# Keys and values on 128 partitions with 64x64 matmul tiles, filler matmuls and a rearranged start, in a kernel of efficient attention followed by a multiplicative feed-forward network

## The chip, the core and the metric

The kernel runs on one core of a Trainium2 chip; the other cores are idle. The metric is the device time of that core in microseconds (us), and a kernel's time is the median of its runs. The kernel before takes 279.56 us (three runs, 279.26 to 280.37). In the profiles, PE is the matrix engine (TensorE), PEld its weight loads, DVE is VectorE, ACT ScalarE, POOL GpSimd, and SP the engine that issues the DMA transfers. One-core kernels have no undisturbed second die to compare with, so a run counts as slow when it is over 1.5% above the fastest run of the same kernel; only fast runs are compared.

## The reference

Eight batches of eight heads with 576 tokens and a head dimension of 64 go through an attention without a token-by-token product: the queries get a softmax over the head dimension, the keys a softmax over the tokens, and `kv` is a 64x64 matrix for each head. Its output (4608 tokens of 512) goes through a feed-forward network of two matrices that are multiplied element by element, and two more matrices after that.

```python
def _attn_ref(q, k, v):                       # [8, 8, 576, 64] float32 each
    q_s = np.exp(q - np.max(q, axis=-1, keepdims=True))
    q_s = q_s / (np.sum(q_s, axis=-1, keepdims=True) + 1e-09)
    k_s = np.exp(k - np.max(k, axis=2, keepdims=True))
    k_s = k_s / (np.sum(k_s, axis=2, keepdims=True) + 1e-09)
    kv = np.einsum('bhsd,bhse->bhde', k_s, v)
    return np.einsum('bhsd,bhde->bhse', q_s, kv)

def _moe_ref(x, w1, w2, w3, w_out):           # x: [4608, 512]
    a = x @ w1                                # [4608, 1024]
    b = x @ w2
    h = a * b @ w3
    return h @ w_out                          # [4608, 512]
```

(Shortened; the types are unchanged.)

## The kernel before

The program is one list of tasks. Each task names its engine, a duration, what it depends on and which buffers it uses. When the kernel is built, a planner simulates all engines with these durations, takes for every engine the task that can start first (with priorities), gives out the buffers, and emits the instructions in that order. The order is then fixed: each engine's queue holds its instructions in the planned order. So a wrong duration or a wrong load rate in the plan does not make a wrong result; it can make an order in which an engine waits for something late while other work would be ready.

The two last matrices are multiplied once into `W3O` (called so below), since `h` is not needed. The first 512 tokens go through the feed-forward network plainly ("the plain group"). The other 4096 tokens are five groups of 2x320 to 2x448 tokens, each multiplied in a scheme with seven instead of eight block products. That needs combinations of the weight blocks (`make_w12`) and of the token blocks (`t_comb`).

Queries, keys and values are loaded on 96 partitions (each holds 6 consecutive tokens of 4 heads), in halves of 4 heads:

```python
    def load_qkv(b, which, hf):
        src = {"q": q, "k": k, "v": v}[which]
        load((which, b, hf), SP * 1536 * 4, 300.0,           # SP = 96, R = 6
             lambda t: t[:SP].rearrange("p (h x) -> p h x", h=4),
             src[b, 4 * hf:4 * hf + 4].rearrange("h (p r) d -> p h (r d)", r=R))
```

`load` takes one of six staging buffers (`st`) of 128x1536 float32, for all loads, weights too. The loads are issued in program order, so a staging buffer that is held long stops everything behind it.

Keys get an exp on ACT, values a cast on POOL, and a batch's `kv` is 24 matmuls of 96 rows with two heads side by side (off-diagonal blocks are computed and thrown away). Queries get an exp on ACT, a sum on DVE, a multiplication on POOL into a further buffer, and a transpose: on PE for the first two batches, by DMA for the others.

```python
            def norm(eq=eq, ds=ds, eqn=eqn):                 # POOL
                nc.gpsimd.tensor_tensor(
                    out=eqn.tile..., in0=eq.tile..., in1=ds.tile[:, 1]..., op=ALU.mult)
        # ...
        def kvm():
            for hf in range(2):
                for g in range(2):
                    ek, v16 = eks[2 * hf + g][1].tile, v16s[hf][1].tile
                    o = 512 * hf + 130 * g
                    for r in range(R):
                        nc.tensor.matmul(
                            pa.tile[:, o:o + 130].rearrange("p (h e) -> p h e", h=2),
                            lhsT=ek[:, r].rearrange("p h d -> p (h d)"),
                            rhs=v16[:, 2 * g:2 * g + 2, r, 0:65],
                            start=(r == 0), stop=(r == R - 1))
```

(`...` marks cuts.) All of attention's PSUM goes through one tile, `tiles("pa", 1, [P, 1024], F32, psum)`. The weight combinations are made on DVE from the float32 staging buffers, so that those stay held until the combinations are done:

```python
        def k1():                                            # sw: float32, 2 buffers
            nc.vector.tensor_tensor(out=s1.tile, in0=a21, in1=a22, op=ALU.add)
        def k2():
            nc.vector.tensor_tensor(out=s2.tile, in0=s1.tile, in1=a11, op=ALU.subtract)
        # k3, k4 on DVE from a11, a12, a21 and s2; k5, k6 copy s1 and s2 to f16 on ACT
        # ...
        tt, ts = t_comb(i, 8.0 * i - 4, "DVE" if i == 1 else "POOL")
```

The softmax here doesn't subtract the row's maximum and nothing guards it: scores larger than these inputs give would overflow.

## Time and profile before

| reading | value | view |
|---|---|---|
| span of the profiled run | 279.1 us | head of the page |
| PE busy, over the whole span | 84% | busy time by engine |
| first matmul of the feed-forward network | 53.2 us | instructions on the tile `px` |
| first matmul of the second token group | 90.2 us | the same |
| from there to the end | 188.9 us | difference |
| last load of queries issued | 165.1 us | instructions of that load |
| chain of waits | 52% PE, 28% DMA | chain of waits |

The first view is from the page of the kernel before: its head, the busy time by engine, and three rows of the span cut into 40 slices of 7 us (PE busy share in tenths, granted clock in tenths, GB/s moved by DMA).

```profile
span 279.1 us, 4087 instructions
...
PE 234.3 (84%) x1344; PEld 122.1 (44%) x1344; DVE 164.2 (59%) x302; ACT 164.0 (59%) x298; POOL 145.2 (52%) x120
...
PE   1586862799946999894999995999999999999992
...
PEclk9999795599995799998899999999999999999999
...
GB/s 246 377 249 257 248 278 173 196 270 264 253 262 311 230 229 236 217 212 244 290 223 282 242 213 243 253 80 40 80 40 42 71 40 75 64 49 74 42 144 120
```

PE is 80 to 100% busy from the second quarter on, with dips. In the slice from 42 to 49 us PE drops to 2, and the clock is at 5 from 42 to 56 us; a second dip (4 and 6) follows from 77 to 91 us, with the clock at 5 in its second half. The loads run at about 250 GB/s until about 180 us, except in the second slice, where only weights are loaded (377), and around 42 to 56 us (173 and 196), where the loads themselves stall.

The next view cuts out four stretches. The columns are the stretch, its length, then for PE, PEld, DVE, ACT and POOL the busy us (and instructions), then the granted clock, the DMA share and GB/s.

```profile
15.00:39.00 24.00, 18.70 (x126) 8.91 (x125) 5.75 (x10) 10.84 (x15) 6.05 (x5) 0.93 1.08 250
42.00:54.00 12.00, 5.07 (x28) 2.72 (x28) 10.89 (x19) 7.88 (x15) 5.73 (x3) 0.52 0.50 165
60.00:63.00 3.00, 3.00 (x15) 1.37 (x14) 3.00 (x6) 3.00 (x6) 0.00 (x0) 1.00 1.09 259
90.20:182.00 91.80, 82.39 (x510) 45.54 (x509) 63.97 (x130) 71.83 (x138) 71.88 (x55) 0.96 1.12 239
```

In the stretch 60 to 63 us only keys and values are loaded, and the DMA is fully busy (share 1.09) at 259 GB/s. From 42 to 54 us the DMA share falls to 0.50 and PE works for 5 of 12 us at half the clock. From 90.2 to 182 us PE is idle for 91.80 - 82.39 = 9.4 us.

The next two views are the shares of the chain that ended last, and the matmuls on the tile `px` (columns: line, engine, operation, tiles and count; shortest, median and longest ns; first and last start in us; shapes). Line 568 is the seven-product scheme, line 509 the plain group.

```profile
PE 52%; DMA 28%; DVE 6%; ACT 4%; issue 4%; POOL 3%; SPq 0%; DVEq 0%; ACTq 0%; POOLq 0%
```

```profile
L568 PE MATMUL px<-xt,w x80: 296/352/474, 90.2 to 258.0; 128*128 128x448 f16 x48, 128*128 128x320 f16 x16, 128*128 128x384 f16 x16
...
L509 PE MATMUL px<-xt,w x32: 379/379/631, 53.2 to 66.5; 128*128 128x512 f16 x32
```

The last view shows three groups of instructions that the change touches (columns: line, engine, operation, tiles, shapes, count; busy us and mean ns of one; idle time of the engine before them and what ended it).

```profile
L306 DVE TENSOR_REDUCE ds<-eq 96x12 f32<-96x768 f16 x32 | 29.8, 930 | 6.7 <-ACT eq L300 6.6
...
L351 PE MATMUL pa<-v,ek 96*128 96x130 f16 x192 | 13.9, 231 | 1.2 <-ACT xt L388 0.7 <-POOL v L289 0.5
...
L544 POOL TENSOR_TENSOR tt<-xt 128x896 f16<-128x896 f16 x6 | 11.2, 1881 | 0.4 <-ACT xt L388 0.4
```

They are the sums of the queries, the kv matmuls (231 ns each in the mean, over 192 of them), and the token combinations on POOL, 1.88 us for one.

### The profile page before, as it was taken

The page shows a single profiled execution, that of the slowest core. Times are in us where ns is not written, and L with a number is a line of the kernel's source. Part 1 is how long each engine was busy: PE and PEld are TensorE (multiplying, and loading weights), DVE is VectorE, ACT ScalarE, POOL GpSimd, SP SyncE. Part 2 cuts the span into 40 slices and gives each one's busy share as a digit, 9 for nine tenths or more (in the row PEclk, how much of TensorE's full clock was granted, in tenths as well). Part 3 has the DMA queues.
Part 4 walks back from the last instruction along what each step waited for, and adds up shares of the span by engine and source line. Part 5 has one row for each costly group of instructions (what it writes and reads, how often), then busy time and mean ns, then how long its engine had stood idle before and what let it go on. Part 6 is the DMA issues. An engine that isn't in the chain of part 4 may idle for free.

```text
span 279.1 us, 4087 instructions
## 1 busy us (share of the span) xinstructions
PE 234.3 (84%) x1344; PEld 122.1 (44%) x1344; DVE 164.2 (59%) x302; ACT 164.0 (59%) x298; POOL 145.2 (52%) x120
## 2 busy tenths in 40 slices
PE   1586862799946999894999995999999999999992
PEld 1232331345424566541464542554544445555540
DVE  1210169983739779671798861898665565555510
ACT  3043546696755769776888685975645444545310
POOL 2213246204566378869869689989694221222200
PEclk9999795599995799998899999999999999999999
DMA  7999995699999999999999999931311212212154
GB/s 246 377 249 257 248 278 173 196 270 264 253 262 311 230 229 236 217 212 244 290 223 282 242 213 243 253 80 40 80 40 42 71 40 75 64 49 74 42 144 120
DMA packets 46037, 52.04 MB, mean 186 GB/s; under 512 B 16832, under 2 KB 39360, under 8 KB 46016
## 3 DMA queue, kind: packets, MB, share of 16 engines
q1 hardware_dynamic: 46016, 51.79, 77.0%
q8 instruction: 10, 0.16, 0.3%
q14 instruction: 11, 0.09, 0.1%
HBM read 38.80 MB, written 9.44 MB: 173 GB/s over the span
## 4 chain that ended last, share of the span: by engine, by line
PE 52%; DMA 28%; DVE 6%; ACT 4%; issue 4%; POOL 3%; SPq 0%; DVEq 0%; ACTq 0%; POOLq 0%
PE px L568 18%; PE pp L634 14%; PE pp L568 13%; DMA st<-in_q_dram 11%; DMA st<-in_moe_w_dram 7%; DMA qsT<-eqn 4%; DMA st<-in_k_dram 3%; PE pa L377 3%; PE pa L351 3%; POOL tt L544 2%; ACT eq L300 2%; DMA out_dram<-osb 2%; DMA st<-in_moe_w_out_dram 1%; ACT xt L388 1%; DVE ds L306 1%
## 5 line engine op out<-in xcount | busy, mean ns | idle before, releaser
L634 PE MATMUL pp<-W3O,ab 128*128 128x512 f16 x288 | 77.7, 379 | 0.8 <-DVE c L593 0.7
L593 DVE TENSOR_TENSOR c<-pp,u 128x448 f16<-128x448 f32 (+2 forms) x80 | 45.6, 575 | 35.3 <-ACT u L589 23.2
L311 POOL TENSOR_TENSOR eqn<-eq,ds 96x768 f16<-96x768 f16 x32 | 49.0, 1541 | 29.4 <-DVE ds L308 17.6
L619 POOL TENSOR_TENSOR ab<-c,c 128x448 f16<-128x448 f16 (+2 forms) x40 | 38.3, 958 | 49.1 <-DVE c L593 48.9
L568 PEld LDWEIGHTS <-wc 128*128 128x128 f16 x320 | 31.6, 99 | 37.6 <-issue 9.2
L568 PE MATMUL px<-tt,wc 128*128 128x448 f16 (+2 forms) x160 | 41.7, 349 | 4.2 <-POOL tt L544 3.9
L634 PEld LDWEIGHTS <-ab 128*128 128x128 f16 x288 | 27.9, 98 | 25.7 <-issue 1.3
L589 ACT COPY u<-px 128x448 f32<-128x448 f32 x48 | 25.5, 537 | 23.0 <-PE px L568 17.1
L289 POOL CAST v<-st 96x1536 f16<-96x1536 f32 x16 | 23.2, 1461 | 26.1 <-DMA st<-in_v_dram 24.6
L306 DVE TENSOR_REDUCE ds<-eq 96x12 f32<-96x768 f16 x32 | 29.8, 930 | 6.7 <-ACT eq L300 6.6
L568 PEld LDWEIGHTS <-w 128*128 128x128 f16 x240 | 23.7, 99 | 21.7 <-issue 1.8
L300 ACT ACTIVATE eq<-st 96x768 f16<-96x768 f32 x32 | 26.1, 842 | 10.9 <-DMA st<-in_q_dram 10.7
L644 ACT ACTIVATE osb<-pp 128x512 f32<-128x512 f32 x33 | 19.4, 600 | 21.0 <-PE pp L634 21.0
L593 DVE TENSOR_TENSOR c<-pp,s 128x448 f16<-128x448 f32 (+2 forms) x40 | 23.0, 579 | 13.7 <-PE pp L568 8.8
L280 ACT ACTIVATE ek<-st 96x768 f16<-96x768 f32 x32 | 26.2, 847 | 8.2 <-DMA st<-in_k_dram 8.2
L388 ACT CAST xt<-pa 128x576 f16<-128x576 f32 (+6 forms) x48 | 21.5, 484 | 8.2 <-PE pa L377 7.7
L593 DVE TENSOR_TENSOR ab<-px,c 128x448 f16<-128x448 f32 (+2 forms) x40 | 23.3, 582 | 5.0 <-PE px L568 2.7
L434 PE MATMUL pp<-ab,ab 128*128 128x512 f16 x64 | 19.0, 436 | 4.1 <-DVE ab L405 1.8
L377 PE MATMUL pa<-qsT,kv 128*128 128x288 f16 x64 | 14.2, 306 | 8.8 <-DVE qsT L332 6.3
L568 PE MATMUL pp<-tt,wc 128*128 128x448 f16 (+2 forms) x80 | 20.5, 341 | 1.1 <-DVE c L593 1.1
L590 ACT COPY u<-px 128x320 f32<-128x320 f32 (+1 forms) x32 | 14.3, 452 | 12.0 <-PE px L568 7.4
L568 PE MATMUL pp<-tt,w 128*128 128x448 f16 (+2 forms) x80 | 20.2, 336 | 0.7 <-DVE c L593 0.7
(52 smaller groups left out, 274.3 us busy)
## 6 DMA issues: line engine op xcount, KB each, us to landing
st<-in_k_dram SPq DMA_DIRECT2D x16, 576.0 KB, 8.2
st<-in_v_dram SPq DMA_DIRECT2D x16, 576.0 KB, 11.1
st<-in_q_dram SPq DMA_DIRECT2D x16, 576.0 KB, 10.7
st<-in_moe_w_dram SPq DMA_DIRECT2D x16, 512.0 KB, 9.6
out_dram<-osb SPq DMA_DIRECT2D x24, 192.0 KB, 2.3
out_dram<-osb SPq DMA_DIRECT2D x24, 128.0 KB, 2.5
st<-in_moe_w_out_dram SPq DMA_DIRECT2D x4, 512.0 KB, 8.2
out_dram<-osb SPq DMA_DIRECT2D x24, 64.0 KB, 2.0
```

The costliest lines, as they stand in the source:

```text
L280: nc.scalar.activation(out=ek.tile.rearrange("p r h d -> p h r d"), in_=vk(bk.tile)[:, 2 * g:2 * g + 2].rearrange("p h (r d) -> p h r d", ...
L289: nc.gpsimd.tensor_copy(out=v16.tile[:, :, :, 0:D], in_=vv(bv.tile).rearrange("p h (r d) -> p h r d", r=R))
L300: nc.scalar.activation(out=eq.tile.rearrange("p r h d -> p h r d"), in_=vq(bq.tile)[:, o:o + 2].rearrange("p h (r d) -> p h r d", r=R), fu ...
L306: nc.vector.tensor_reduce(out=ds.tile[:, 0], axis=AX.X, op=ALU.add, in_=eq.tile.rearrange("p r h d -> p (r h) d"))
L311: nc.gpsimd.tensor_tensor(out=eqn.tile.rearrange("p r h d -> p (r h) d"), in0=eq.tile.rearrange("p r h d -> p (r h) d"), in1=ds.tile[:, 1] ...
L377: nc.tensor.matmul(xp.tile[:, 224 + hh * HS:224 + (hh + 1) * HS], lhsT=kv2.tile[:, p, :], rhs=qsT.tile.rearrange("p r s -> p (r s)")[:, hh ...
L388: nc.scalar.copy(out=xt_buf[i].tile[:, p, lo - starts[i]:hi - starts[i]], in_=xp.tile[:, 224 + lo - b * S:224 + hi - b * S])
L568: nc.tensor.matmul(ps.tile[:, 0:h], lhsT=lhs(c), rhs=rhs(c), start=first and c == 0, stop=c == 1, skip_group_check=not first)
L589: return lambda: nc.scalar.copy(out=dst.tile, in_=src.tile[:, 0:h]) if h == HM else \
L593: return lambda: nc.vector.tensor_tensor(out=dst(), in0=ps.tile[:, 0:h], in1=other.tile[:, 0:h], op=op)
L619: nc.gpsimd.tensor_tensor(out=ab.tile[:, 0:h], in0=c11.tile[:, 0:h], in1=c21.tile[:, 0:h], op=ALU.mult)
L634: nc.tensor.matmul(po.tile, lhsT=ab_buf[(i, ft)].tile[:, tb * P:(tb + 1) * P], rhs=W3O[ft], start=(ft == 0), stop=(ft == N_FT - 1))
```

## The change

The intent: the loads of keys and values shall run faster by using all 128 partitions (2 heads x 64 groups of 9 tokens), so that the attention is earlier; and the start shall be shortened by releasing staging buffers and PSUM earlier. In seven parts:

1. Keys and values on 128 partitions, and with that `kv` as 72 matmuls of 64x64 array tiles (two heads lie on the lower and the upper half of the partitions and go to the lower and the upper half of PSUM).
2. Two PSUM tiles of one bank for attention instead of one of two banks; batch 0 also uses tiles of the feed-forward network, and half of its copies go to DVE.
3. Weight combinations from the f16 weights, on DVE alone.
4. All token combinations on DVE.
5. The normalisation of the queries in place, more buffers (`eq`, `ek`, `st`, `v16`), queries in staging buffers of their own.
6. Another load order: W3O's matrices alternate, queries come before keys and values.
7. Filler matmuls: where the plan sees PE wait in its first 65 us, it inserts matmuls on zeros.

```diff
+    def load_kv(b, which, hf):
+        src = {"k": k, "v": v}[which]
+        load((which, b, hf), P * 1152 * 4, 385.0, lambda t: t.rearrange("p (a x) -> p a x", a=2),
+             src[b, 4 * hf:4 * hf + 4].rearrange("(a t) (g r) d -> (t g) a (r d)", t=2, r=RK))   # RK = 9
 ...
-                    o = 512 * hf + 130 * g
-                    for r in range(R):
-                        nc.tensor.matmul(
-                            pa.tile[:, o:o + 130].rearrange("p (h e) -> p h e", h=2),
-                            lhsT=ek[:, r].rearrange("p h d -> p (h d)"),
-                            rhs=v16[:, 2 * g:2 * g + 2, r, 0:65],
-                            start=(r == 0), stop=(r == R - 1))
+                        o = 65 * (2 * hf + g)
+                        for r in range(RK):
+                            for i in range(2):
+                                sl = slice(64 * i, 64 * i + 64)
+                                nc.tensor.matmul(
+                                    pa.tile[sl, o:o + 65], lhsT=ek[sl, r, :],
+                                    rhs=v16[sl, g, r, 0:65], start=(r == 0), stop=(r == RK - 1))
 ...
-    tiles("pa", 1, [P, 1024], F32, psum)
+    tiles("pa", 2, [P, 512], F32, psum)
 ...
-            def norm(eq=eq, ds=ds, eqn=eqn):
+            def norm(eq=eq, ds=ds):
                 nc.gpsimd.tensor_tensor(
-                    out=eqn.tile.rearrange("p r h d -> p (r h) d"),
+                    out=eq.tile.rearrange("p r h d -> p (r h) d"),
 ...
+        def comb(o, a, b, op):
+            return lambda: nc.vector.tensor_tensor(out=o, in0=a, in1=b, op=op)
+        n1 = add("DVE", d, comb(wc[:, 0], w2[:, 0:2], w2[:, 2:4], ALU.add), [t2], [], pc)
+        n2 = add("DVE", d, comb(wc[:, 1], wc[:, 0], w1[:, 0:2], ALU.subtract), [n1, t1], [], pc + 0.1)
 ...
-        tt, ts = t_comb(i, 8.0 * i - 4, "DVE" if i == 1 else "POOL")
+        tt, ts = t_comb(i, 8.0 * i - 4, "DVE")
 ...
+            if e == "PE" and self.filler and free[e] < self.filler[0]:
+                n = int((s - free[e] - 60) / 113)
+                spare = [x for p in self.filler[1] for x in self.pools[p] if x[0] <= free[e]]
+                if n >= 3 and spare:
+                    order.append((free[e], len(order), Fill(self.filler[2], spare[0][2], n)))
 ...
+    def fill(ps, n):
+        for _ in range(n):
+            nc.tensor.matmul(ps[:, 0:256], lhsT=blank[:, 0:P], rhs=blank, start=True, stop=True)
+    plan.filler = (65000.0, ("pp", "pa", "px"), fill)
```

## The prediction

> **What bounds the kernel now.** The windows view shows three stages. (a) 0 to 53 us: start-up. TensorE waits for loads and for the first batch's attention; the timeline has the first feed-forward matmul at 53.2 us. DMA share is about 1.05 from 9 to 42 us, then falls to 0.1-0.6 from 45 to 54 us: float32 weight combinations hold staging buffers, and four transpose-copy-matmul-copy rounds of 2.7 us share one PSUM tile. (b) 57 to 180 us: DMA share 1.06-1.2 throughout, mostly q/k/v loads at 230-262 GB/s. TensorE still idles about 16 us here (81-87, 114-117, 123-132, 168-175 us); the second token group starts only at 90.2 us. (c) 183 us to the end: DMA share 0.2-0.4, TensorE 100% busy. The chain of waits: 52% PE, 28% DMA.
>
> **What the change does.**
> - k and v on 128 partitions. Loads of 96 partitions run at 250-262 GB/s at share 1.07-1.10; the 128-partition weight loads at 3-12 us ran at 340-410 at share 0.95-1.04. The Trainium skill, "SBUF — State Buffer", section on the DMA port swizzle, puts partitions 0-63 on eight ports and 64-127 on the other eight, so 96 partitions load one half with 2/3 of the bytes: an estimated 0.75 of the full rate, and the trace agrees (about 255 against 345). Estimate: one batch's loads fall from 3.54 MB/255 = 13.9 us to 4.6 (q) + 6.8 (k, v) = 11.5 us; eight batches save 19 us of DMA.
> - kv as 72 matmuls of 64x64 tiles instead of 24 of 96x128 (1.40 us per batch). I expect about 2.6 us (estimate: 64-column weight loads at half the measured 100 ns, partly overlapped): +7 us of TensorE over the batches that matter.
> - Weight combinations in f16 on VectorE (about 0.3 instead of 0.68 us, no ScalarE copies, staging freed at the cast); token combinations off POOL (1.88 us each) to VectorE (about 0.5 us each): removes the 123-132 us hole.
> - Two one-bank PSUM tiles for attention, query loads first: the 45-54 us serial rounds shrink by about 6 us.
> - Filler matmuls in the first 65 planned us. The granted clock is 0.50 at 45-54 and 84-93 us, after idle stretches, as the skill's "TensorE: Matmul & The Clock Gate", Part 1, says of idle beyond a window of about 3.4 us. Worth 2-4 us at most; badly timed fillers cost 1-2.
> - Query norm in place: deeper buffers, no time by itself.
>
> **Sum.** Loads up to the last w1/w2 quarter: 10.5 MB/345 + 1.2/255 + 2.4/345 + 2.5 = 44 us (before: about 57). First feed-forward matmul at 40 us (-13); second group at about 70 us (-20), after 30 us of TensorE work (plain group, its output, late W3O, attention). The rest takes 189 us now; minus 8 of idle, plus 6-7 for kv tiles: 187-188. 70 + 188 = **258 us**, range 250 to 267. Chances: faster by over 2% 0.96, within 2% 0.03, slower 0.01.
>
> **What would show the steps right or wrong.** k/v loads above 320 GB/s while they run; DMA share falling by about 160 us instead of 180; first feed-forward matmul near 40 us; second group near 70 us; kv block 2-2.7 us; clock above 0.9 before 60 us.
>
> **What would make it wrong.** The kv tiles not overlapping (4 us a batch, +10 us); planned order not matching real landing times, so in-order ScalarE or TensorE queues block on a later batch's load, as at 82.6 us now; VectorE (already 90% in places) becoming the limit; fillers delaying real work.

## The result, and the profile after

| | before | after |
|---|---|---|
| median of the runs | 279.54 us (four runs) | 260.36 us (four runs: 259.13, 263.57, 261.59, 256.32) |
| span of the profiled run | 279.1 us | 257.3 us |
| first matmul of the feed-forward network | 53.2 us | 37.0 us |
| first matmul of the second group | 90.2 us | 66.4 us |
| from there to the end | 188.9 us | 190.9 us |
| PE idle in the middle | 9.4 us (90.2 to 182) | 12.3 us (66.4 to 162) |
| last load of q, k or v issued | 165.1 us | 140.4 us |

The ratio is 0.9215, with a 95% interval from 0.9123 to 0.9307. A ratio here is the mean time of one kernel's fast runs over that of the other kernel's fast runs in the same rounds, so it is not quite the ratio of the quoted medians. The changed kernel was run once more in later rounds as a control (e11 below) and gave 0.9221. Its runs scatter over 7 us. The kernel before scattered by 1 us in these runs, but from 277.26 to 285.12 us in the later rounds; what sets the scatter was not found. The second and third run are marked slow and are left out of the ratio.

The same views as before, for the changed kernel. First the page:

```profile
span 257.3 us, 5030 instructions
...
PE 234.6 (91%) x1820; PEld 126.5 (49%) x1820; DVE 175.7 (68%) x331; ACT 151.8 (59%) x312; POOL 109.4 (43%) x103
...
PE   8999889969689989699799797999999999999991
...
PEclk9999999997999999799999999999999999999998
...
GB/s 256 404 328 348 399 383 286 356 209 360 220 210 383 101 307 311 334 261 292 274 293 181 381 134 46 48 85 72 50 43 42 82 41 84 41 52 71 63 149 118
```

The deep dips of PE are gone (its lowest slices ahead of the last are at 6), and the clock is at 9 in all slices but two of 7 and the last. The load rates in the first 65 us are mostly 280 to 400 GB/s; before they were mostly 170 to 280. From about 150 us the traffic falls off; before, that point came at about 180 us. Note that PE's 1344 instructions became 1820: the kv tiles add 384, the fillers the other 92.

```profile
15.00:39.00 24.00, 22.33 (x231) 13.26 (x230) 15.72 (x35) 13.76 (x24) 10.01 (x8) 1.00 1.07 360
42.00:54.00 12.00, 11.88 (x74) 5.38 (x74) 11.66 (x24) 9.56 (x15) 4.09 (x3) 1.00 1.04 291
60.00:63.00 3.00, 2.94 (x12) 1.18 (x11) 2.90 (x6) 2.77 (x7) 1.81 (x2) 0.77 1.05 406
66.40:162.00 95.60, 83.33 (x837) 46.30 (x836) 81.81 (x152) 73.82 (x170) 60.05 (x50) 0.98 0.91 247
```

From 60 to 63 us keys and values now load at 406 GB/s. The stretch 15 to 39 us went from 250 to 360 GB/s. In the middle, 66.4 to 162 us, DVE is busy for 81.81 of 95.6 us (86%); in the middle of the kernel before it was 63.97 of 91.8 us (70%). PE is idle for 95.60 - 83.33 = 12.3 us there.

```profile
PE 55%; DVE 18%; DMA 15%; ACT 5%; issue 4%; SPq 1%; DVEq 0%; ACTq 0%
```

```profile
L567 PE MATMUL px<-xt,w x80: 296/352/353, 66.4 to 236.3; 128*128 128x448 f16 x48, 128*128 128x320 f16 x16, 128*128 128x384 f16 x16
...
L508 PE MATMUL px<-xt,w x32: 376/379/381, 37.0 to 51.8; 128*128 128x512 f16 x32
```

DMA fell in the chain from 28 to 15%, but DVE rose from 6 to 18%. The landmarks moved by 16.2 and 23.8 us.

```profile
L322 DVE TENSOR_REDUCE ds<-eq 96x12 f32<-96x768 f16 x32 | 29.6, 925 | 3.9 <-ACT eq L316 3.8
...
L370 PE MATMUL pa<-v,ek 64*64 64x65 f16 x576 | 11.8, 197 | 1.3 <-POOL v L305 1.3
...
L543 DVE TENSOR_TENSOR tt<-xt 128x896 f16<-128x896 f16 x6 | 6.0, 1026 | 1.9 <-ACT xt L410 1.8
```

The kv matmuls take 11.8 us in sum instead of 13.9, although there are three times as many. The sums of the queries are unchanged. A first token combination takes 1.03 us on DVE in the mean.

Two of the waits of PE (total us, times, longest us) show where DVE enters:

```profile
PE pa L396 <- DVE kv L380: 6.8, 7, 1.8
PE px L567 <- DVE tt L543: 3.6, 3, 2.1
```

PE waits 6.8 us for the normalised kv and 3.6 us for token combinations, both from DVE. In the kernel before, the largest wait of PE in the middle was another:

```profile
PE px L568 <- POOL tt L544: 3.9, 2, 2.5
```

Asked for the middle alone (90.2 to 182 us), the waits of PE in the kernel before are 3.9 us for POOL, 2.4 for DVE, 1.3 for ACT and 1.1 for a transpose by DMA; none of them is directly for a load. In the changed kernel (66.4 to 162 us) 10.9 us are for DVE, 6.2 of them for the normalised kv, and 1.2 for ACT. The timeline shows why PE waits for kv: after each of the six kv blocks there, DVE starts the normalisation only 0.9 to 2.3 us after the block's end, and is busy with other work until then. In the kernel before it started within 0.3 us after five of six blocks, and after 0.96 us once.

**Where the time came from.** The span fell by 21.8 us. The start of the second group moved forward by 23.8 us, and the rest of the kernel became 2.0 us longer. So all of the gain lies before 66 us; the later part lost a little, in spite of the faster loads that it also has. The two later parts can be compared: PE is busy in them for 174.2 and 173.1 us. DVE's work there rose from 117.9 to 132.4 us, and POOL's fell from 111.1 to 82.9.

### The profile page after: what moved, and what is told of

It reads as the page before. It is cut to its first block, busy times and chain, and to the rows that moved or that the text cites. A ratio compares the mean times of both kernels' runs of the same rounds, so it can differ in the third digit from the quotient of the medians.

```text
span 257.3 us, 5030 instructions
## 1 busy us (share of the span) xinstructions
PE 234.6 (91%) x1820; PEld 126.5 (49%) x1820; DVE 175.7 (68%) x331; ACT 151.8 (59%) x312; POOL 109.4 (43%) x103
## 4 chain that ended last, share of the span: by engine, by line
PE 55%; DVE 18%; DMA 15%; ACT 5%; issue 4%; SPq 1%; DVEq 0%; ACTq 0%
PE pp L633 19%; PE px L567 16%; PE pp L567 12%; DMA st<-in_moe_w_dram 10%; DVE tt L543 4%; DMA sq<-in_q_dram 4%; DVE ds L322 4%; DVE c L592 4%; PE pp L712 4%; PE pa L396 3%; DVE kv L380 2%; DMA out_dram<-osb 2%; DVE ab L592 1%; ACT xt L410 1%; ACT eq L316 1%
## 5 line engine op out<-in xcount | busy, mean ns | idle before, releaser
L633 PE MATMUL pp<-W3O,ab 128*128 128x512 f16 x288 | 80.8, 384 | 0.3 <-DVE c L592 0.2
L618 POOL TENSOR_TENSOR ab<-c,c 128x448 f16<-128x448 f16 (+2 forms) x40 | 39.4, 985 | 81.5 <-DVE c L592 80.4
L327 POOL TENSOR_TENSOR eq<-eq,ds 96x768 f16<-96x768 f16 x32 | 47.1, 1487 | 33.9 <-DVE ds L324 25.6
L567 PE MATMUL px<-tt,wc 128*128 128x448 f16 (+2 forms) x160 | 40.2, 339 | 3.8 <-DVE tt L543 3.6
L322 DVE TENSOR_REDUCE ds<-eq 96x12 f32<-96x768 f16 x32 | 29.6, 925 | 3.9 <-ACT eq L316 3.8
L316 ACT ACTIVATE eq<-sq 96x768 f16<-96x768 f32 x32 | 26.0, 842 | 7.9 <-DMA sq<-in_q_dram 7.9
L410 ACT CAST xt<-pa 128x288 f16<-128x288 f32 (+6 forms) x72 | 23.0, 380 | 12.6 <-PE pa L396 12.5
L567 PE MATMUL px<-xt,wc 128*128 128x448 f16 (+2 forms) x80 | 20.2, 335 | 1.2 <-ACT u L589 1.2
L298 ACT ACTIVATE ek<-st 128x576 f16<-128x576 f32 x32 | 21.0, 691 | 0.0
L567 PE MATMUL pp<-xt,w 128*128 128x448 f16 (+2 forms) x80 | 20.8, 342 | 0.0
L567 PE MATMUL px<-xt,w 128*128 128x448 f16 (+2 forms) x80 | 20.0, 336 | 0.2 <-DVE ab L592 0.2
```

The lines of the kernel that those rows point to most:

```text
L298: nc.scalar.activation(out=ek.tile.rearrange("p r d -> p (r d)"), in_=vk(bk.tile)[:, g], func=AF.Exp)
L316: nc.scalar.activation(out=eq.tile.rearrange("p r h d -> p h r d"), in_=vq(bq.tile)[:, o:o + 2].rearrange("p h (r d) -> p h r d", r=R), fu ...
L322: nc.vector.tensor_reduce(out=ds.tile[:, 0], axis=AX.X, op=ALU.add, in_=eq.tile.rearrange("p r h d -> p (r h) d"))
L327: nc.gpsimd.tensor_tensor(out=eq.tile.rearrange("p r h d -> p (r h) d"), in0=eq.tile.rearrange("p r h d -> p (r h) d"), in1=ds.tile[:, 1][ ...
L410: (nc.vector.tensor_copy if by_dve else nc.scalar.copy)(out=xt_buf[i].tile[:, p, lo - starts[i]:hi - starts[i]], in_=xp.tile[:, lo - base: ...
L567: nc.tensor.matmul(ps.tile[:, 0:h], lhsT=lhs(c), rhs=rhs(c), start=first and c == 0, stop=c == 1, skip_group_check=not first)
```

## The experiments

Twelve kernels were run. The question was which of the seven parts brought the 20 us, and why the later part brought nothing. My theory was that the rate of the k and v loads is most of it, and that DVE took over as the limit in the later part. The rivals were: that released staging buffers and PSUM brought it, that the fillers did, and, for the later part, that the order of the plan or the one PSUM path limits it, not the engines. Each expectation below was on record before its kernel ran; "theory" there is as each text defines it.

### e1: no filler matmuls

```diff
-    plan.filler = (65000.0, ("pp", "pa", "px"), fill)
```

> The changed kernel (260.4 us) without the filler matmuls, all else equal. My theory (start-up is bound by loads; the fillers only keep the clock up): 2 to 4 us slower, 262 to 264; the first feed-forward matmul at 38 to 39 us instead of 37.0, granted clock 0.5 to 0.7 in some windows before 60 us. Rival (the fillers carry the start-up gain): first feed-forward matmul after 43 us and total above 267. Third possibility (fillers delay real work): equal or faster.

Measured: 260.05 us (258.85 to 261.13), ratio 0.9257 (0.917 to 0.9343). The interval overlaps that of the changed kernel (0.9123 to 0.9307). The first feed-forward matmul starts at 38.4 us instead of 37.0 and the second group at 65.7 instead of 66.4. The clock is 0.70 from 30 to 40 us (1.00 in the changed kernel), so the fillers do what they are made for.

What follows: the fillers keep the clock up and are worth nothing that these runs can show. A worth of 1 to 2 us is not excluded: the mean of e1's fast runs is 260.0 us, that of the changed kernel's 257.7 (two runs) and 258.4 (three runs of e11).

### e2: the changed kernel with keys and values back on 96 partitions

```diff
-        load((which, b, hf), P * 1152 * 4, 385.0, lambda t: t.rearrange("p (a x) -> p a x", a=2),
-             src[...].rearrange("(a t) (g r) d -> (t g) a (r d)", t=2, r=RK))
+        load((which, b, hf), SP * 1536 * 4, 290.0, lambda t: t[:SP]...,
+             src[...].rearrange("h (p r) d -> p h (r d)", r=R))
-    # kv: 72 matmuls of 64x64 tiles into one pa tile
+    # kv: 24 matmuls of 96x128 into two pa tiles, each normalised by itself
```

(With the staging and `ek`, `v16` buffers in the shapes that this needs: 5 staging buffers, 5 `ek`, 3 `v16`.)

> The changed kernel with keys and values on 96 partitions as before (same bytes of staging: 5 wider buffers for 7; kv in 24 full-width matmuls over two PSUM tiles). My theory (loads on 128 partitions are the main gain): k and v loads fall back to about 255 GB/s, the first two batches arrive about 5 us later, the load stage ends near 175 us instead of 155, total 266 to 272. Rival (after the other edits VectorE paces the middle stage, so the layout hardly matters): the loads slow just as much but the total is under 264.

Measured: 280.12 us (278.81 to 283.66), ratio 0.9957 (0.9857 to 1.0057): in the total the whole gain is gone. The first feed-forward matmul starts at 42.3 us and the second group at 79.2 us; loads run at 210 to 240 GB/s, and the last load of values is issued at 177.4 us. The profiled run is the one marked slow (283.66), so these moments are rough. It has one wait that neither kernel has (total us, times, longest):

```profile
PE pa L402 <- DMA qsT<-eq: 10.5, 2, 9.3
```

PE waits 9.3 us at once for a transpose by DMA: the plan put five of them in a row. This belongs to the rearranged plan, not to the layout as such.

What follows: without the layout the other six parts are worth nothing in the total, in this plan. At the start they are worth something even so: the second group comes at 79.2 us, 11 us earlier than in the kernel before, and the part after it takes 202.7 us instead of 188.9 (both from the slow run). The 20 us cannot all be put down to the load rate, as about 9 of them stand in one wait that the new plan made. There is a further difference, not tested apart: the kv of 96 partitions here takes both of attention's PSUM banks at once, and e8 and e10 below lose about 5 and 7 us where these banks are short. The next experiment goes the other way.

### e3: the kernel before with the layout only

```diff
+        if which != "q":
+            load((which, b, hf), P * 1152 * 4, 385.0,
+                 lambda t: t[:, :1152].rearrange("p (a x) -> p a x", a=2),
+                 src[b, 4 * hf:4 * hf + 4].rearrange("(a t) (g r) d -> (t g) a (r d)", t=2, r=RK))
+            return
 ...
+    # ek, v16, kvm, kvn as in the changed kernel; ek 6 and v16 4 buffers (the same bytes as before)
```

> The kernel before (279.5 us) with only keys and values on 128 partitions and the 64x64 tiles. My theory: load stage shorter by about 17 us, total 266 to 272. Rival (start-up serial rounds and token combinations on POOL hold it up): loads speed up the same but the total stays above 274. The kv block should take about 1.5 us per batch in either case, as the changed kernel's trace shows, not the 2.6 us of the prediction.

Measured: 268.62 us (267.82 to 269.55), ratio 0.9564 (0.9483 to 0.9645). The second group starts at 78.0 us, 12 us earlier than in the kernel before:

```profile
L570 PE MATMUL px<-xt,w x80: 296/352/474, 78.0 to 245.2; 128*128 128x448 f16 x48, 128*128 128x320 f16 x16, 128*128 128x384 f16 x16
```

Two stretches of it (columns as above):

```profile
12.00:24.00 12.00, 11.53 (x70) 5.42 (x69) 3.34 (x6) 6.68 (x11) 3.33 (x4) 1.00 1.03 415
36.00:42.00 6.00, 2.97 (x22) 1.83 (x22) 5.16 (x10) 4.74 (x11) 3.79 (x2) 0.50 0.34 112
```

From 12 to 24 us the loads run at 415 GB/s. But from 36 to 42 us the DMA share is 0.34: the loads stand still, because the float32 weight combinations hold the staging buffers, and PE is half idle at half the clock.

What follows: the layout alone is worth about 4.4% (12 us), a little more than half of the change. The rest of the gain needs the staging buffers free.

### e7: e3 with the weight combinations of the changed kernel

```diff
-        n1 = add("DVE", dve(512), k1, [ta, tb], [s1, ba, bb], prio + 1)
+        n1 = add("DVE", d, comb(wc[:, 0], w2[:, 0:2], w2[:, 2:4], ALU.add), [t2], [], pc)
 ...   # all of make_w12 as in the changed kernel
```

> The kernel before with the 128-partition keys and values and the f16 weight combinations, nothing else. The layout alone gave 268.6 us, with DMA share down to 0.35 at 36 to 42 us while staging buffers were held. If the f32 combinations hold them: the hole closes, second group at 73 to 75 us instead of 78, total 264 to 266. If the attention rounds through one PSUM tile are what holds the start-up: no change, 267 to 270.

Measured: 262.74 us (fast runs 262.27, 262.03 and 263.2; one of 267.09), ratio 0.9334 (0.9253 to 0.9416). The same stretch and the same landmark as in e3:

```profile
36.00:42.00 6.00, 3.08 (x18) 1.56 (x17) 4.70 (x9) 3.57 (x7) 4.42 (x2) 0.50 1.09 387
```

```profile
L550 PE MATMUL px<-xt,w x80: 296/352/578, 72.7 to 239.1; 128*128 128x448 f16 x48, 128*128 128x320 f16 x16, 128*128 128x384 f16 x16
```

The DMA share from 36 to 42 us is 1.09 instead of 0.34, at 387 GB/s, and the second group starts at 72.7 us instead of 78.0. From there to the end it takes 187.8 us, as before (188.9) and in e3 (188.2).

What follows: combinations from the f16 weights are worth 2.3 points (6 us). They release the staging buffers at the cast, and the loads go on; DVE's busy time in the stretch hardly changes (4.70 instead of 5.16 us). That it is only this, and not also the shorter DVE work and the missing copies on ACT, was not tested apart. Layout and combinations together are 6.7 of the change's 7.8 points. (This kernel ran in other rounds than e3, each against the kernel before.)

### e4: token combinations of the groups 2 to 5 back on POOL

```diff
-        tt, ts = t_comb(i, 8.0 * i - 4, "DVE")
+        tt, ts = t_comb(i, 8.0 * i - 4, "DVE" if i == 1 else "POOL")
```

> The changed kernel with the token combinations of groups 2 to 5 back on POOL. My prediction's step (they leave a hole of some 5 us at a group's start on POOL): 4 to 8 us slower, 264 to 268, with TensorE waits for tt on POOL back in the chain. Rival (VectorE is the limit of the middle stage in the changed kernel, 85 to 95 per cent busy): within 2 us of it or faster, the work moved off VectorE paying for the later tt.

Measured: 260.57 us (258.01 to 262.28), ratio 0.9214 (0.9091 to 0.9336), the same as the changed kernel. PE waits for token combinations from both engines now:

```profile
PE px L567 <- POOL tt L543: 2.7, 1, 2.7
PE px L567 <- DVE tt L543: 2.2, 1, 2.2
```

That is 4.9 us in sum; with all on DVE it was 3.6.

What follows: moving them brought nothing in total. In the kernel before, POOL's combinations stood in the chain for 5.56 us at 125 us; here, in the changed order, the longest such wait is 2.7 us, and that for DVE is 2.2. The run also says something about DVE. In its middle (67.2 to 163 us) DVE is busy for 72.38 of 95.8 us (76%), 9.4 us less than in the changed kernel, and POOL for 75.84; yet PE is idle for 12.8 us and still waits 4.7 us for the normalised kv. So relieving DVE alone by this much, at POOL's cost, does not shorten the later part.

### e5: the loads alone

A kernel that only loads, without any arithmetic on the data, and then stores zeros. Its output is wrong, which doesn't matter for the time. Seven series of 12 loads, on six staging buffers.

```diff
+    for i in range(N):
+        part96(q, i)          # 96 partitions, pieces of 6 tokens of a head (1536 bytes)
+    # then: 96 partitions in pieces of 3072 bytes; 128 partitions in pieces of 2304 bytes (as the change);
+    # 128 in pieces of 1536; weights (128, 4096); 96 and weights in turn; 128 and weights in turn
```

> Loads alone, a wrong result on purpose: seven stretches of 12 transfers, always six in flight, then the output filled with zeros. In order: (1) queries as the kernels load them, 96 partitions in runs of 1536 B; (2) 96 partitions, runs of 3072 B; (3) 128 partitions, runs of 2304 B, as the changed kernel loads keys and values; (4) 128 partitions, runs of 1536 B; (5) weight rows, 128 partitions, 4096 B; (6) form 1 and weights in turn; (7) form 3 and weights in turn. Theory A (the number of partitions sets the rate): 1 and 2 both at 240 to 270 GB/s, 3, 4 and 5 at 380 to 420, 6 near 270 to 300 because the even half of the partitions stays the bottleneck, 7 at 400. Theory B (the length of the runs sets it): 2 above 350, 4 near 260, 6 near the mean of 1 and 5.

Measured, in one run of 175.7 us (its state is unknown, as it is single). The view shows each series' inner stretch (columns here: stretch, length, DVE, POOL, granted clock, DMA share, GB/s):

```profile
6.00:26.00 20.00, 0.00 (x0) 0.00 (x0) 1.00 1.10 250
32.00:54.00 22.00, 0.00 (x0) 0.00 (x0) 1.00 1.03 260
60.00:74.00 14.00, 0.00 (x0) 0.00 (x0) 1.00 1.06 392
78.00:92.00 14.00, 0.00 (x0) 0.00 (x0) 1.00 1.06 373
97.00:108.00 11.00, 0.00 (x0) 0.00 (x0) 1.00 1.03 410
112.00:130.00 18.00, 0.00 (x0) 0.00 (x0) 1.00 1.07 305
133.00:141.00 8.00, 0.00 (x0) 0.00 (x0) 1.00 1.04 400
```

In this order: 96 partitions 250 GB/s, with longer pieces 260; 128 partitions 392, with shorter pieces 373; weights 410; 96 and weights in turn 305; 128 and weights in turn 400.

What follows: the number of partitions decides, and the length of a contiguous piece does not (10 and 19 GB/s between short and long). The DMA share is 1.03 to 1.10 throughout, so the share does not show that 96 partitions load slowly: it tells that the engines are occupied, not how well. The mixed series had been expected at 270 to 300 by the first theory; 305 is just the mean by bytes of 250 and 410 (an estimate from the two: 1,114,112 bytes in 589,824/250 + 524,288/410 gives 306). The second theory had said "near the mean", but its other two numbers failed. So a slow load does not slow its neighbours beyond its own time. And the ratio 250/392 = 0.64 is lower than the 0.75 of the prediction.

### e6: the kv tiles not alternating

```diff
-                        for r in range(RK):
-                            for i in range(2):
+                        for i in range(2):
+                            for r in range(RK):
```

> The changed kernel with the two 64x64 tiles of a head pair one after the other (nine matmuls on the first tile, then nine on the second) instead of in turn. If the tiles work at the same time only when they alternate, the kv block of 72 matmuls grows from 1.34-1.5 us to 2.4-3 us and the total by 4 to 10 us; if the 21 ns per matmul come from somewhere else (issue), the block stays at 1.3 to 1.5 us and the total within 3 us of 260.

Measured, one look (state unknown): 258.06 us, as fast as the changed kernel. The timeline of one undisturbed kv block (start, duration, engine, line, tiles, count), first of this kernel, then of the changed kernel:

```profile
87.00 1.79 PE L370 MATMUL pa<-v,ek 64*64 64x65 f16 x72
```

```profile
87.59 1.34 PE L370 MATMUL pa<-v,ek 64*64 64x65 f16 x72
```

That is 1.79/72 = 24.9 ns for a matmul in the serial order, and 1.34/72 = 18.6 ns when two tiles alternate. The start times in the packed traces show more. In the changed kernel the starts come in pairs, one for each tile: the second follows mostly after 3 to 4 ns (286 of the 566 gaps within the blocks are under 10 ns), the next pair after 29 ns more (median). In the serial order a quarter of the gaps (148 of 566) are still under 10 ns, so the two tiles overlap there too, in part.

What follows: two tiles do overlap, and they start almost together when they alternate; the change of order costs 0.45 us a block, which is less than the whole worth of the overlap. The expected 2.4 to 3 us of the serial order was wrong: I had costed a 64-column weight load and matmul too high. Eight blocks, 3.6 us, made no difference that one run shows.

### e8: one PSUM bank for attention

```diff
-    tiles("pa", 2, [P, 512], F32, psum)
+    tiles("pa", 1, [P, 512], F32, psum)
```

> The changed kernel with one PSUM bank for attention instead of two. If the two banks carried the rest of the start-up gain (my theory): second group 3 to 6 us later, total 263 to 267. If they do not: within 2 us of 260.

Measured: 267.1 us in the median (262.54 to 271.66), ratio of the fast runs (two of four) 0.9397 (0.928 to 0.9514). The profiled run (268.0) is marked slow, so the two lines that follow are taken with care; but the ratio, from fast runs, shows a loss of the same kind.

```profile
L567 PE MATMUL px<-xt,w x80: 296/352/582, 76.1 to 245.2; 128*128 128x448 f16 x48, 128*128 128x320 f16 x16, 128*128 128x384 f16 x16
```

```profile
PE pa L396 <- DVE kv L380: 14.4, 8, 3.0
```

What follows: the second bank is worth about 1.8 points (5 us). In the slow profile all of the loss lies at the start: the second group comes 10 us later, and from there to the end it is 190.1 us, no longer than with two banks. In it the wait of PE for the normalised kv doubles (14.4 us instead of 6.8), which suggests that this wait comes from how the attention's steps pass through PSUM as well as from DVE's load; no fast profile was taken to confirm it.

### e9: the queries on 128 partitions too

This follows from e5 and from DVE's new place in the chain. Queries in the layout of keys and values load faster, and the same numbers on 128 instead of 96 partitions make every instruction on them shorter: one exp, one sum and one normalisation of 128x1152 per half batch in place of two of 96x768. The kv of a head then goes from row tile t to column tile a, so that its output lies on the partitions where the transposed queries are.

```diff
-        load(("q", b, hf), SP * 1536 * 4, 290.0, ..., "h (p r) d -> p h (r d)", "sq")
+        load(("q", b, hf), P * 1152 * 4, 385.0, ..., "(a t) (g r) d -> (t g) a (r d)", "sq")
 ...
-        for p in range(4):                    # eq [96, 6, 2, 64]: exp, sum, norm, transpose
+        for hf in range(2):                   # eq [128, 9, 2, 64]: the same, once per half
 ...
+                            for t in range(2):                          # kv
+                                a = t ^ x
+                                nc.tensor.matmul(pas[t].tile[so, o:o + 65], lhsT=ek[sl, r, :],
+                                                 rhs=v16[sl, a, r, 0:65], ...)
 ...
+                            nc.tensor.matmul(                           # x, in 64x64 tiles
+                                xps[a].tile[st, 0:HS]..., lhsT=kv2.tile[sa, 2 * t + hf, :],
+                                rhs=qsT.tile[sa, r0:r1, st], start=True, stop=True)
```

A first draft let both row tiles write the same PSUM bank. The author reports that the race check refused it before any run ("two matmuls from different row tiles write the same PSUM bank quadrant"; the refusal itself is not in the record); in the version that ran, each row tile has a bank of its own, one of them from the feed-forward network's pool.

> The changed kernel carried further: queries too on 128 partitions (2 heads x 64 groups of 9 tokens), the product with kv in 64x64 tiles, so that no zero-padded kv is needed; one exponential, one sum and one normalization of 128x1152 per half batch instead of two of 96x768. Two PSUM banks per kv block and per product, one from the attention pool and one from the feed-forward pool. My theory (loads at 250 GB/s of the queries and VectorE set the start of the second group and the idle TensorE in the middle): query loads at about 390 GB/s, 8 times 1.18 MB x (1/250 - 1/390) = 1.7 us per batch less DMA; VectorE sum 1.3 us per half batch instead of 2 x 0.93; second group at 62 to 64 us; total 247 to 254. If PSUM contention or tile switching eats it: 256 to 262.

Measured: 242.46 us (242.36 to 242.59), ratio 0.8652 (0.857 to 0.8735). Against the changed kernel in the same rounds (e11) it is 242.47/258.44 = 0.938 (means of the fast runs). The result is correct.

```profile
L577 PE MATMUL px<-xt,w x80: 298/352/363, 58.8 to 219.6; 128*128 128x448 f16 x48, 128*128 128x320 f16 x16, 128*128 128x384 f16 x16
```

```profile
58.80:140.00 81.20, 77.07 (x854) 39.33 (x852) 68.00 (x134) 66.69 (x148) 49.37 (x39) 1.00 0.99 279
```

```profile
L320 DVE TENSOR_REDUCE ds<-eq 128x18 f32<-128x1152 f16 x16 | 21.4, 1339 | 0.1
```

The second group starts at 58.8 us, and from there to the end it takes 181.6 us, 9 us less than in the changed kernel and 6 less than in e7, the shortest so far. In the middle PE is idle for 81.20 - 77.07 = 4.1 us, and PE is 95% busy over the whole span. The sums of the queries take 21.4 us in place of 29.6, and all that touches the queries shrinks alike: exp 18.4 us in place of 26.0, normalisation 33.8 in place of 47.1 (groups of instructions).

What follows: this beats both kernels by far, and it is the first version in which the later part becomes shorter. Load rate and engine time change together in it, and attention also gets PSUM banks from the feed-forward pool, so it does not tell which of them does it. That is for e10 (the banks) and e12 (the engines). (The automatic verdict over these later rounds, e9 to e12, was "unclear" for all of them; many of the runs of the kernel before were slow there. The intervals, from fast runs alone, all end below 0.95.)

### e10: e9 with both attention banks from attention's own pool

```diff
-        pas = [pa, Buf("pp")]
+        pas = [pa, Buf("pa")]
```

(And the same for the bank pair of the product with the queries.)

> As e9, with both banks of each pair from the attention pool (two banks in all, so kv and products follow one another). More serial attention, less pressure on the feed-forward banks. If the one-bank result of e8 (7 us lost) carries over: 3 to 7 us slower than e9; if the feed-forward banks are what is short: faster than e9.

Measured: 249.06 us (248.39 to 250.08), ratio 0.889 (0.8815 to 0.8964); the second group starts at 63.5 us.

What follows: 6.6 us slower than e9, within the 3 to 7 that were expected. With a pair of banks for each step, the pool of two holds one step only. The second group starts 4.7 us later than in e9, and the rest takes 184.8 us instead of 181.6. So the banks from the feed-forward pool are a part of e9's gain over the changed kernel.

### e11: the changed kernel once more

> The changed kernel once more, on the same chip as e9 and e10, to compare them with it directly: 257 to 263 us.

Measured: 259.35 us in the median (fast 259.3, 259.4 and 256.62; slow 261.16), ratio 0.9221 (0.911 to 0.9333).

What follows: the result repeats, and the scatter too.

### e12: e9 with the saved engine work put back

The loads stay as in e9. A useless exp, sum and copy of half a tile bring ScalarE, VectorE and POOL back to about the busy time that the 96-partition layout gives them. The plan is not told, so the extra work comes at moments that it did not foresee.

```diff
+                nc.scalar.activation(out=eq.tile[:, :, 0], in_=vq(bq.tile)[:, 0]..., func=AF.Exp)
                 nc.scalar.activation(...)                       # the real exp
+                nc.vector.tensor_reduce(out=ds.tile[:, 0, 0:RK], axis=AX.X, op=ALU.add,
+                                        in_=eq.tile[:, :, 0])
                 nc.vector.tensor_reduce(...)                    # the real sum
+                nc.gpsimd.tensor_copy(out=eq.tile[:, :, 0], in_=eq.tile[:, :, 0])
```

> The kernel of e9 (242.5 us) with the engine time that its wider queries saved put back as useless work on the same data, plan and loads unchanged: per half batch one more sum over half the tile on VectorE (about 0.67 us against 0.69 saved), one more exponential of half the tile on ScalarE (about 0.6 against 0.5 saved) and one copy of half the tile on POOL. If the faster query loads gave e9 its gain over the changed kernel: within 3 us of 242.5. If the relief of the engines, VectorE above all, gave it: 249 to 257. In between: both.

Measured: 256.88 us (256.64 to 259.65), ratio 0.9249 (0.9071 to 0.9428).

```profile
L583 PE MATMUL px<-xt,w x80: 297/352/363, 63.0 to 234.1; 128*128 128x448 f16 x48, 128*128 128x320 f16 x16, 128*128 128x384 f16 x16
```

```profile
63.00:160.00 97.00, 85.83 (x884) 42.76 (x883) 81.81 (x151) 76.44 (x166) 60.23 (x52) 0.98 0.79 226
```

```profile
L325 DVE TENSOR_REDUCE ds<-eq 128x18 f32<-128x1152 f16 x16 | 21.6, 1353 | 0.5
...
L323 DVE TENSOR_REDUCE ds<-eq 128x9 f32<-128x576 f16 x16 | 11.8, 740 | 0.7 <-ACT eq L317 0.7
```

The extra sums (line 323) are 740 ns each, 11.8 us in all; the extra exps 686 ns each (11.0 us), the copies on POOL 665 ns each (10.6 us). From the second group to the end it takes 191.9 us again, and PE is idle for 97.00 - 85.83 = 11.2 us in the middle, as in the changed kernel (12.3).

What follows: with the fast query loads and e9's PSUM banks kept and the engine work put back, 14.4 us of e9's gain are gone: the ratio is 0.9249, that of the changed kernel in e11 (other rounds) 0.9221, and the medians are 256.88 and 259.35 us. So neither faster query loads nor the banks keep the gain without the relief of the engines. Three limits of this. The put-back work is unplanned, and larger than what was saved on DVE (11.8 against 29.6 - 21.4 = 8.2 us) and on ACT (11.0 against 7.6), smaller on POOL (10.6 against 13.3), so it may cost more than the real work did, and the 2.5 us between the medians are no upper bound for the loads. Over the whole kernel DVE is busy for 174.1 us, as in the changed kernel (175.7). It loads all three engines at once, so it does not show which of them matters. And PE's idle time comes back with other waits: 0.8 us for the normalised kv (6.2 in the changed kernel's middle), 4.0 for token combinations, 1.4 for other DVE work and 3.7 for ACT.

## Why the prediction was right, and where it was wrong

The predicted time was 258 us, in a range from 250 to 267; measured were 260.4. The total is right, and so is the first of its two terms. The second term was wrong in both of its parts, which cancelled, and that is luck: neither the 8 us of idle to be removed nor the 6 to 7 us of added kv time was there. What was left of the errors cancelled as well: the second group came 3.6 us earlier than predicted, and the rest took 3 us longer.

**Landmarks at the start (predicted 40 and 70 us): right, a little too careful.** Measured were 37.0 and 66.4 us. e3 and e7 show the mechanism that was named: the layout brings the second group from 90.2 to 78.0 us, the freed staging buffers to 72.7, and the second PSUM bank with the rest to 66.4 (e8, one bank less: 76.1, in a slow run). The two one-bank tiles were predicted to save about 6 us; e8 puts the second bank at about 5.

**Rate of k and v (predicted 345 GB/s): mechanism right, size too small.** The estimate took 0.75 from the arithmetic of ports in the page that it names: with 96 partitions, 2/3 of the bytes go to the half of the ports that serves partitions 0 to 63. e5 measured 250 against 392 GB/s, 0.64. The prediction had also taken the low end of the 340 to 410 GB/s that it had read from the first weight loads; e5 gives 410 for them. The end of the load stage was predicted at 160 us and came at about 150.

**kv tiles (predicted 2.6 us a batch, +7 us): failed.** An undisturbed block takes 1.34 us (1.40 before), and the mean over all eight is 11.8/8 = 1.5 us, less than the 13.9/8 = 1.7 us of before. The term of +6 to 7 us in the sum did not exist. It was made up from half of a 128-column weight load's time for each matmul (36 ns); the trace has 18.6, as two tiles start 3 to 4 ns apart. e6 shows that even without the alternation the block would be 1.79 us.

**8 us of idle removed from the later part: failed.** The later part is 190.9 us, 2.0 longer than before. PE's idle time in the middle did not fall: 9.4 us before, 12.3 after. The prediction's reasoning was that faster loads end the holes. But none of PE's own waits in the middle of the kernel before was directly for a load (8.7 us in all, 3.9 of them for POOL's token combinations). In the changed kernel DVE ends most of PE's waits: its share of the chain rose from 6 to 18%, and the waits of PE for DVE in the middle are 10.9 us. This was named under "what would make it wrong" (VectorE becoming the limit), and in the trace it happened, only without harm to the total, as the kv term was wrong the other way. e9 and e12 show that this part depends on the work of the engines that prepare the attention: less of it gives 181.6 us, unplanned work put in its place gives 191.9 us with the loads still fast. That it is DVE's work alone is not shown, and e4, which takes 9.4 us off DVE in the middle without effect, speaks against it.

**Token combinations "about 0.5 us on VectorE": too small, and without effect.** The first pair's mean is 1026 ns. e4 shows no difference in total whether DVE or POOL makes them.

**Weight combinations: right in kind.** The prediction wrote 0.3 us instead of 0.68, and that staging is freed at the cast. They take about 0.42 us; e7 puts the whole of it at 6 us, and its trace shows the loads going on with the staging freed.

**Fillers 2 to 4 us at most: nothing that is clear of the scatter.** e1 shows the clock to be 0.70 without them at 30 to 40 us, and no change in time that these runs resolve. The slow clock that the prediction cites is in the trace (0.52 from 42 to 54 us before), but the idle stretches before it are shorter than the window of about 3.4 us that it names: the clock fell at 42.4 and 83.4 us, and in the 3.4 us before that PE was busy for 1.2 and 0.8 us. The slow stretches lasted 13.7 and 10.2 us, four and three times 3.4. With the fillers the clock still fell once before 66 us (0.80 in the mean of 55 to 60 us).

**What stays open.** How much of e2's loss of 20 us is the load rate, how much its unlucky plan and how much its use of both PSUM banks; what the load order, the queries' own staging buffers and the deeper buffers are worth, which no run takes apart; whether the layout alone (e3) gains from the shorter exp and cast (847 to 691 ns, 1461 to 1168 ns) as well as from the rate; which of DVE, ACT and POOL limits the later part; why the rate of 96 partitions is 0.64 and not 0.75 of that of 128; and what makes the changed kernel's runs scatter.

## What to carry to other kernels

Put data on all 128 partitions before anything else: here it raised a load's rate from 250 to 392 GB/s and shortened the elementwise instructions about in proportion (the sums of the queries from 29.6 to 21.4 us). Both effects come together in e3 (12 us) and in e9 (17 us, with more PSUM banks), and e12 shows for the queries that the second cannot be left out. A buffer's holding time, not its producer's speed, can be the cost of a slow step in a chain of loads: look for stretches in which the DMA share falls while loads are still to come. And when one limit is removed from a stage, do not subtract its idle time from the total: look up which engine stands at 80% right behind it, and test the engines one at a time, by giving each less work or useless work.

## What the Trainium skill lacked or had wrong

- "SBUF — State Buffer", section "Door 1: The DMA port swizzle", gives the ports of 32, 64 and 128 partitions but no value for 96. An estimate from its two halves of eight ports gives 0.75 of the full rate; the loads alone measured 250 against 392 GB/s, 0.64. It gives no reason for the rest. The length of the contiguous piece is not it: 250 and 260 GB/s at 1536 and 3072 bytes on 96 partitions, 373 and 392 at 1536 and 2304 bytes on 128.
- "DMA: Bandwidth & Descriptors", section "Where 436 GB/s comes from", says that the memory side, about 358 GB/s for a core, binds for transfers between HBM and SBUF. With one core busy, weights came at 410 GB/s over 11 us, and the mixed loads of e3 at 415 over 12 us, so it did not bind here. The page itself, just above, gives about 358 for two cores of one memory that load at once; only this section's sentence lacks that condition.
- "TensorE: Matmul & The Clock Gate", Part 1, states that matmuls start no closer than about 25 ns however small they are. As it stands this is too wide: with two row tiles alternating, the trace has most starts of a pair 3 to 4 ns apart, and then 29 ns to the next pair. Part 3 of the same page has the former, about 4 ns from tile to tile.
- "TensorEngine Tiling (Array Packing)", "Gotcha 1: PSUM Pressure", says that different row tiles cannot access one PSUM bank simultaneously. The changed kernel's two row tiles alternate in one bank on different partition halves, 576 matmuls in all, in pairs that start mostly 3 to 4 ns apart, with a correct result; so the sentence is too wide. The page "PSUM — Partial Sum Buffer", in its section on bank collisions, puts the limit at one bank and one quadrant of 32 partitions, which fits.
- No page describes a test by useless work for the case that none of the engines that prepare the data is full: in e12 DVE was busy for 81.81 of 97 us, ACT for 76.44 and POOL for 60.23, and yet the work put on these three cost about 14 us.
